# Two places where VectorE reads a sum: a change to the order of a fused attention and MLP kernel

## The chip, the cores and the metric

The kernel runs on one core of a Trainium2 chip. A core has five engines that run side by side, each with a queue of its own: TensorE (PE) multiplies matrices and writes into PSUM, VectorE (DVE) and ScalarE (ACT) read PSUM, GpSimd (POOL) works on the on-chip memory SBUF alone, and SyncE (SP) here only issues transfers. The metric is the device time of one execution in microseconds (us), lower being better; the medians of several runs are compared. A profile is one further execution, recorded instruction by instruction.

## What is computed

One transformer block with adaptive layer norm: 2048 tokens of width 512, 32 query heads of width 16 that share one key and one value head, and an MLP of inner width 1376. Everything is float32 to the caller.

```python
mod = silu(c) @ w_mod                        # six rows of 512: sa, ca, ga, sb, cb, gb
h = layernorm(x) * (1 + ca) + sa
q, k, v = h @ wq, h @ wk, h @ wv             # 32 heads of 16; one k, one v
p = softmax(q k^T / 4)                       # 32 x 2048 x 2048
x = x + ga * ((p v) @ wo)
h = layernorm(x) * (1 + cb) + sb
x = x + gb * (gelu(h @ w1 + b1) @ w2 + b2)
```

## The kernel before

**Units and passes.** The 2048 tokens are cut into eight blocks of 256, and each block into eight units of four heads, which makes 64 units. The loop at the end of the program goes through the units, with four passes for each unit: 256 passes in all. For one unit the softmax needs the row maximum first (a pass over all scores with nothing kept but the maximum) and the exponentials second. Both are made in the same loop, for different units: while unit u has its exponentials made, the maxima of a unit some way ahead are found.

**What a pass issues.** A pass has two half cycles. Each half cycle issues, in one order written by hand: four max products `m` (TensorE, 64 rows of the array, 512 columns, `Max.step`, L490), each followed by its reduction on VectorE (`mx`, L493); four score products `e` (L561), each followed by an exponential on ScalarE (`p`, L562); and the halves of the products of one filling batch (below, L183). Behind each half cycle stand sixteen small products `acc` that multiply the exponentials by the values (L573). In the first half cycle of a pass the max products use rows 64 to 127 of the array and the filling batch rows 0 to 63, and in the second the other way round, so that two products run side by side in the two halves of the array.

**PSUM banks.** The max products have three banks (`tag="m"`), the score products three (`e0` to `e2`), the accumulated `acc` one (`v`), and the filling products one (`x`). With one bank for the filling products, a new sum cannot start until the finished one has been read out of it.

**Filling batches.** All that is not attention is cut into batches that ride along in the half cycles. `take()` hands out a batch of up to twelve products; the batch is issued twice, half its contraction in each half cycle of the pass (`half`, L177 and L183). A sum is closed by a batch whose last product carries the stop flag (`batch[-1][4]`), and opened by one whose first product carries the start flag (`batch[0][3]`). There are five kinds of sums: query projections (`qps`, two batches, read by a VectorE copy, L441), output projections (`wops`, two batches, read by VectorE, L761), transposes (`tp`, one batch of four, read by a VectorE copy, L823, or by ScalarE, L828), the first MLP matrix (`w1ps`, one batch of twelve products of 256 columns, read by VectorE into `z`, L876) and the second (`w2ps`, six batches, read by VectorE, L928). When the last batch of a sum has been issued in the second half cycle, `resume()` (L1314) lets the job go on, and the job then issues the instruction that reads the finished sum. The reading instruction stands on VectorE's queue where `resume()` is called.

**Where the order comes from.** `issue()` takes several lists of steps with lengths, and always issues the step whose list has come least far. `mixture()` puts two lists alternately into one. `halves()` gives each product of a batch the length `ahead`, 0.75 for a full batch, and (6 - 0.5) / total for a smaller one, where total is the batch's size in products of 512 columns. A half cycle that opens a sum has an order of its own in the first half of a pass (the branch `if batch and batch[0][3]`, L1296 to L1300): two score products go first, and the max products follow each other more closely, while the batch starts later. All other half cycles with a batch use the order below it (L1302 and L1303).

**The maxima.** A unit's 32 max products are spread over four passes. After the last one, `put_max` (L504) finds the maximum of each row over its four columns (`mm`, L537), transposes it on VectorE (`turned`, L538), has GpSimd split it in two parts (`mt`, `mh`, `ml`, L532) and sends it with four transfers on SP's queue into the unit's query tile `qst` (L527); the score products of that unit wait for it. Time in the program is counted by `clock`, four ticks a pass. `later(n, fn)` puts a step off by n ticks; the transfers are issued four ticks after the reduction. Before the change the reduction itself is put off by `(0 - clock) % 4 + 1` ticks (L543), so it always stands behind the first half cycle of a pass.

Of the kernel before, what the change touches and what calls it, by code (L numbers as in the profile page):

```python
# [11 lines left out]
ALU = mybir.AluOpType  # L12
AX = mybir.AxisListType
# [19 lines left out]
BATCH = 6  # L33
# [14 lines left out]
def adaln_mqa_mlp(  # L48
# [416 lines left out]
    class Max:  # L465
# [14 lines left out]
        def has(self, s):  # L480
            return bool(self.todo[s])

        def step(self, s, **place):
            u, j, t, kc = self.todo[s].pop(0)
            T = blocks[units[u][0]][1] // P
            if u not in self.mx:
                self.mx[u] = att.tile([P, 4 * T, NKC], F32, name=f"mx{u}", tag="mx", bufs=2)
            m = psum.tile([P, 512], F32, name=f"m{u}_{j}_{t}_{kc}_{s}", **(place or dict(tag="m", bufs=3)))
            rows = slice(64 * s, 64 * s + 64)
            nc.tensor.matmul(m, qsts[u][rows, j, t * P:(t + 1) * P], ks[rows, kc * 512:(kc + 1) * 512],  # L490
                             start=True, stop=True)
            i = (s * 2 + j) * T + t
            nc.vector.tensor_reduce(out=self.mx[u][:, i, kc:kc + 1], in_=m, axis=AX.X, op=ALU.max)  # L493
            self.done += 1
            self.left[u] -= 1
            if self.left[u] == size[u] // 2 and u > 1 and u + 1 < NU:
                load_q(u + 1)
            if self.left[u] == 0:
                put_max(u, self.mx.pop(u))

    placed = set()
    mms = []
# [1 line left out]
    def put_max(u, mx):  # L504

        T = blocks[units[u][0]][1] // P
        qst = qsts[u]
        if not mms:  # L510
            for i in range(2):
                mms.append(att.tile([P, 32], F32, name=f"mm{i}"))
                nc.gpsimd.memset(mms[i], 0.0)
        mm = mms[u % 2]
        turned = att.tile([P, 32], F32, name=f"turned{u}", tag="turned", bufs=2)
        if u == 0:
            pad(att, 256, "pad7")
        mt = att.tile([4 * T, P], F32, name=f"mt{u}", tag="mt", bufs=2)
        mh = att.tile([4 * T, P], F32R, name=f"mh{u}", tag="mh", bufs=2)
        ml = att.tile([4 * T, P], F32R, name=f"ml{u}", tag="ml", bufs=2)  # L520

        def send():
            for s in range(2):
                for r, src in ((48, mh), (49, ml)):
                    dst = qst[64 * s + r:64 * s + r + 1].rearrange("p j (t n) -> p (j t) n", n=P)
                    ring = nc.scalar if u == 0 and s else nc.sync
                    ring.dma_start(out=raw(dst), in_=raw(src[2 * T * s:2 * T * (s + 1), :].unsqueeze(1)))  # L527
            placed.add(u)

        def gather():  # L530
            for g in range(0, P, 32):
                nc.gpsimd.tensor_scalar(out=mt[:, g:g + 32], in0=turned[g:g + 4 * T, :], scalar1=1.0, scalar2=0.0,  # L532
                                        op0=ALU.mult, op1=ALU.add)
            split(mh, ml, mt, nc.gpsimd, nc.gpsimd)

        def reduce():
            nc.vector.tensor_reduce(out=mm[:, :4 * T], in_=mx, axis=AX.X, op=ALU.max)  # L537
            nc.vector.transpose(out=turned, in_=mm)  # L538
            later(MAX_WAIT[0], gather)
            later(MAX_WAIT[1], send)  # L540


        later((0 - clock[0]) % 4 + 1, reduce)  # L543

    ptiles = {}
    accs = {}
# [527 lines left out]
    def resume():  # L1074

        go_on(holder[0])
# [187 lines left out]
    for u in range(NU):  # L1264
        for K in range(0, steps[u], 2):
            goal = lead[u] + (lead[u + 1] - lead[u]) * (K + 2) / steps[u]
            goal = min(goal, first[u + QBUFS] if u + QBUFS < NU else first[NU])
            n = max(0, 2 * round((goal - mp.done) / 2))

            def maxes(s, n, first_=1.0):  # L1270
                return [(1.0 if i else first_, lambda: mp.step(s)) if mp.has(s) else (0.0, lambda: None) for i in range(n)]

            def exps(s, which):
                return [(1.0, lambda K=K, j=j, bank=bank: sexp(u, K, j, s, bank)) for K, j, bank in which]

            def halves(batch, s):

                total = products(batch)
                ahead = AHEAD if total > BATCH - 0.5 else (BATCH - 0.5) / total
                return [(ahead * products([one]), lambda one=one: half(one, s)) for one in batch]  # L1280

            def plain(s, K, t, n, banks):

                a, b_, c_, d = banks
                one = mixture(exps(s, [(K, 0, a), (K, 1, c_)]), maxes(s, n))
                other = maxes(t, n)
                if not holder and mp.has(t) and n > 1:
                    other[-1] = 1.0, lambda: mp.step(t, tag="x", bufs=1)
                issue(one, exps(t, [(K, 0, b_)]) + other + exps(t, [(K, 1, d)]))

            X, Y = K, K + 1
            due()
            batch = take() if behind else None
            if batch and batch[0][3]:  # L1296

                one = mixture(maxes(1, n // 2), exps(1, [(X, 0, 1), (X, 1, 2)]))
                issue(one, exps(0, [(X, 0, 0)]) + halves(batch, 0))
                issue(exps(1, [(Y, 0, 0)]))  # L1300
            elif batch:
                issue(mixture(maxes(1, n // 2, 0.0), exps(1, [(X, 0, 0), (X, 1, 1), (Y, 0, 2)])),  # L1302
                      halves(batch, 0) + exps(0, [(X, 0, 0)]))  # L1303
            else:
                plain(1, X, 0, (n + 2) // 4, (1, 2, 0, 1))
            clock[0] += 1
            due()
            if behind:
                end_step(*behind)
            clock[0] += 1  # L1310
            due()
            if batch:
                issue(mixture(maxes(0, n // 2, 0.0), exps(0, [(X, 1, 0), (Y, 0, 1), (Y, 1, 2)])),
                      halves(batch, 1) + [(0.0, resume)] + exps(1, [(Y, 1, 0)]))  # L1314
                advance()
            else:
                plain(1, Y, 0, n // 4, (2, 0, 1, 2))
            clock[0] += 1
            due()
            end_step(u, X)  # L1320
            behind = (u, Y)
            clock[0] += 1
            if state["mods"] and state["q"] == 0 and w2H is None:
                w2H = att.tile([P, NF, D], F32R, name="w2H", tag="bigH")
                w2L = att.tile([P, NF, D], F32R, name="w2L", tag="bigL")
                preps["w2"] = prep_w2()
            if clock[0] >= prepared[0] + PREP and weights and weights[0] in preps:
                prepared[0] = clock[0]
                if next(preps[weights[0]], 0) == 0:
                    weights.pop(0)  # L1330
# [51 lines left out]
```

## Time and profile before

| | us |
|---|---|
| median of 3 runs | 1605.31 |
| lowest and highest of them | 1603.88, 1605.53 |
| the profiled execution, its own time | 1604.68 |
| its span, first to last instruction | 1602.5 |
| granted TensorE clock, mean | 0.995 of full speed |
| half cycles in its loop | 512 |

A row of the profile that groups instructions gives line, engine, operation, what is written and read, shapes, how many, then the busy time in all, the mean of one in ns, and the engine's idle time before them with the instruction that ended it. A row of a timeline gives the start in us from the span's start, the length, the engine, the operation and how many have been merged into the row; a bracket gives the idle time of that engine before the row and what ended it. PEld is TensorE's loading of weights, which overlaps its products, and waits of a product are mostly seen there. A row of a window table gives the window, its length, the busy time of each engine with its instructions, then the granted clock.

### The profile page before, as it was taken

The numbers are of one execution on the slowest core, as the hardware profiler recorded it, in microseconds if no ns is written. First come the engines' busy times: TensorE is split into PE (matmuls) and PEld (weight loads), VectorE is DVE, ScalarE is ACT, GpSimd is POOL, SyncE is SP. The second block draws the span as 40 slices with busy tenths as digits, with TensorE's granted clock in tenths as the row PEclk, the third lists the DMA queues.
The fourth block names the chain that finished last, engine by engine and source line by source line (L and its number), as shares of the span: only waits on it lengthen the run. The fifth ranks groups of instructions, "written<-read, shape, count | busy, mean of one in ns | idle before, by whom it ended". The sixth has DMA issues, their size and how long they took to land.

```text
span 1602.5 us, 41474 instructions
## 1 busy us (share of the span) xinstructions
PE 1572.6 (98%) x16369; PEld 1018.9 (64%) x16369; DVE 1407.6 (88%) x2473; ACT 1213.7 (76%) x2393; POOL 666.6 (42%) x1176
## 2 busy tenths in 40 slices
PE   6999999999999999999999999999999999999998
PEld 3466665557665666657666676657666676656667
DVE  6899999899999998999989998899999998999615
ACT  5577777678777887778877887778877887778853
POOL 4445444647422571246421462244612473225711
PEclk8999999999999999999999999999999999999999
DMA  7236312313021220303112120302112120212231
GB/s 251 80 108 212 108 68 71 125 32 107 16 94 35 67 68 26 101 19 106 32 50 78 53 84 22 106 14 97 42 40 86 45 95 19 100 33 63 80 134 72
DMA packets 83126, 121.63 MB, mean 76 GB/s; under 512 B 19614, under 2 KB 56222, under 8 KB 82676
## 3 DMA queue, kind: packets, MB, share of 16 engines
q1 hardware_dynamic: 82916, 118.97, 22.6%
q8 instruction: 130, 2.13, 0.6%
q14 instruction: 64, 0.52, 0.1%
q10 hardware_dynamic: 16, 0.00, 0.0%
HBM read 91.13 MB, written 27.27 MB: 74 GB/s over the span
## 4 chain that ended last, share of the span: by engine, by line
PE 90%; DVE 6%; ACT 2%; DMA 1%; issue 0%; POOL 0%; SPq 0%; ACTq 0%; DVEq 0%; POOLq 0%
PE acc L573 30%; PE m L490 25%; PE e L561 17%; PE w1ps L183 7%; DVE mx L493 4%; PE w2ps L183 3%; PE w2ps L177 1%; PE qps L183 1%; PE wops L183 1%; PE w1ps L177 1%; ACT p L562 1%; PE kps L159 1%; PE tp L183 1%; ACT h L828 0%; PE modr L279 0%
## 5 line engine op out<-in xcount | busy, mean ns | idle before, releaser
L493 DVE TENSOR_REDUCE mx<-m 128x1 f32<-128x512 f32 x2048 | 1273.2, 681 | 118.4 <-PE m L490 92.1
L562 ACT ACTIVATE p<-e 128x512 f32<-128x512 f32 x2048 | 1070.7, 600 | 289.4 <-PE e L561 220.5
L490 PE MATMUL m<-ks,qst 64*128 64x512 f32 x2048 | 812.7, 428 | 6.1 <-ACT ks L393 2.4
L561 PE MATMUL e<-qst,ks 64*128 64x512 f32 x2048 | 740.9, 413 | 6.7 <-DMA qst<-ml 5.2
L573 PE MATMUL acc<-p,va 128*32 128x256 f32 x8192 | 548.5, 385 | 0.0
L490 PEld LDWEIGHTS m<-ks,qst 64*128 64x128 f32 x2048 | 362.8, 184 | 226.1 <-DVE mx L493 108.5
L561 PEld LDWEIGHTS e<-qst,ks 64*128 64x128 f32 x2048 | 352.3, 184 | 85.4 <-ACT p L562 56.2
L573 PEld LDWEIGHTS acc<-p,va 128*32 128x32 f32 x8192 | 214.0, 109 | 223.2 <-issue 119.9
L183 PE MATMUL w1ps<-h2H,w1t 64*128 64x256 f32 x1232 | 228.9, 282 | 0.0
L532 POOL TENSOR_SCALAR mt<-turned 8x32 f32<-8x32 f32 x256 | 53.4, 208 | 400.7 <-DVE turned L538 388.7
L183 PEld LDWEIGHTS w1ps<-h2H,w1t 64*128 64x128 f32 x1232 | 189.3, 185 | 0.0
L183 PE MATMUL w1ps<-h2L,w1t 64*128 64x256 f32 x616 | 169.5, 275 | 0.0
L183 PE MATMUL w2ps<-w2H,gL 64*128 64x512 f32 x286 | 118.4, 414 | 0.0
L183 PE MATMUL w2ps<-w2L,gH 64*128 64x512 f32 x286 | 117.2, 410 | 0.0
L183 PE MATMUL w2ps<-w2H,gH 64*128 64x512 f32 x286 | 115.8, 405 | 0.0
L183 PEld LDWEIGHTS w1ps<-h2L,w1t 64*128 64x128 f32 x616 | 113.8, 185 | 0.0
L881 POOL TENSOR_SCALAR tt<-tt 128x256 f32<-128x256 f32 x77 | 31.2, 405 | 164.3 <-ACT tt L880 95.0
L134 POOL TENSOR_TENSOR gL<-z,gH 128x256 fp32r<-128x256 f32 x77 | 56.9, 739 | 6.4
L882 POOL TENSOR_TENSOR tt<-tt,z 128x256 f32<-128x256 f32 x77 | 56.8, 737 | 6.4
L892 POOL TENSOR_TENSOR z<-tt,z 128x256 f32<-128x256 f32 x77 | 56.2, 730 | 6.0
L891 POOL TENSOR_TENSOR tt<-tt,z 128x256 f32<-128x256 f32 x77 | 56.4, 732 | 0.0
L183 PEld LDWEIGHTS w2ps<-w2H,gH 64*128 64x128 f32 x286 | 52.8, 184 | 0.6
(188 smaller groups left out, 1461.2 us busy)
## 6 DMA issues: line engine op xcount, KB each, us to landing
w1t<-dw SPq DMA_DIRECT2D x82, 512.0 KB
qst<-dq SPq DMA_DIRECT2D x384, 32.0 KB
do<-oc SPq DMA_DIRECT2D x64, 128.0 KB
dw<-w1s SPq DMA_DIRECT2D x11, 512.0 KB
xt<-in_A_x_dram SPq DMA_DIRECT2D x4, 1024.0 KB
dq<-qH SPq DMA_DIRECT2D x16, 256.0 KB
dq<-qL SPq DMA_DIRECT2D x16, 256.0 KB
x<-in_A_x_dram SPq DMA_DIRECT2D x8, 512.0 KB
```

The costliest lines, as they stand in the source:

```text
L134: eng_l.tensor_tensor(out=dst_l, in0=src, in1=raw(dst_h), op=ALU.subtract)
L177: nc.tensor.matmul(ps, a, b_, start=first_, stop=last_)
L183: nc.tensor.matmul(ps, a[rows], b_[rows], start=first_ and s == 0, stop=last_ and s == 1)
L490: nc.tensor.matmul(m, qsts[u][rows, j, t * P:(t + 1) * P], ks[rows, kc * 512:(kc + 1) * 512], start=True, stop=True)
L493: nc.vector.tensor_reduce(out=self.mx[u][:, i, kc:kc + 1], in_=m, axis=AX.X, op=ALU.max)
L532: nc.gpsimd.tensor_scalar(out=mt[:, g:g + 32], in0=turned[g:g + 4 * T, :], scalar1=1.0, scalar2=0.0, op0=ALU.mult, op1=ALU.add)
L561: nc.tensor.matmul(e, ks[rows, kt * P:(kt + 1) * P], rhs, start=True, stop=True)
L562: nc.scalar.activation(ptiles[u, K][:, j, s, :], e, AF.Exp, scale=0.25)
L573: nc.tensor.matmul(accs[u][32 * cidx:32 * cidx + 32, :], va[:, kt, :], rhs, start=kt == 0, stop=kt == NKT - 1)
L882: nc.gpsimd.tensor_tensor(out=tt, in0=tt, in1=z, op=ALU.mult)
L891: nc.gpsimd.tensor_tensor(out=tt, in0=tt, in1=z, op=ALU.mult)
L892: nc.gpsimd.tensor_tensor(out=z, in0=tt, in1=z, op=ALU.add)
```

## The change

Three things are changed.

1. The order of its own for a half cycle that opens a sum is taken out. Such half cycles now use the order of all the others.
2. In the second half cycle of a pass whose batch closes a sum, the reduction of the third max product (index 2) is not issued with its product but held, and issued after `resume()`. VectorE's order in that half cycle was: reductions 1, 2, 3, reading of the sum, reduction 4. Now it is: reductions 1, 2, reading of the sum, reductions 3, 4. For small closing batches (the transposes) `ahead` becomes (6 - 1.5) / total, so that `resume()` comes ahead of the fourth max product; there the reading stood behind all four reductions before. What hung on the held reduction (loading the next query tile, `put_max`) goes along with it.
3. For the units of the first two blocks (`u < 2 * NQ`, sixteen units), the reduction in `put_max` is issued at once and not put off. What follows it (GpSimd's split, the transfers) keeps its distance in ticks and so moves ahead with it, by three ticks. From the third block on nothing changes there.

```diff
-        def step(self, s, **place):
+        def step(self, s, hold=None, **place):
...
-            nc.vector.tensor_reduce(out=self.mx[u][:, i, kc:kc + 1], in_=m, axis=AX.X, op=ALU.max)
+
+            def reduce():
+                nc.vector.tensor_reduce(out=self.mx[u][:, i, kc:kc + 1], in_=m, axis=AX.X, op=ALU.max)
+                self.left[u] -= 1
+                if self.left[u] == size[u] // 2 and u > 1 and u + 1 < NU:
+                    load_q(u + 1)
+                if self.left[u] == 0:
+                    put_max(u, self.mx.pop(u))
+
             self.done += 1
...
+            if hold is None:
+                reduce()
+            else:
+                hold.append(reduce)
...
-        later((0 - clock[0]) % 4 + 1, reduce)
+        if u < 2 * NQ:
+            reduce()
+        else:
+            later((0 - clock[0]) % 4 + 1, reduce)
...
-            def maxes(s, n, first_=1.0):
-                return [(1.0 if i else first_, lambda: mp.step(s)) if mp.has(s) else (0.0, lambda: None) for i in range(n)]
+            def maxes(s, n, first_=1.0, held=None):
+                return [(1.0 if i else first_, lambda i=i: mp.step(s, held if i == 2 else None)) if mp.has(s) else (0.0, lambda: None)
+                        for i in range(n)]
...
-                ahead = AHEAD if total > BATCH - 0.5 else (BATCH - 0.5) / total
+                ahead = AHEAD if total > BATCH - 0.5 else (BATCH - (1.5 if batch[-1][4] else 0.5)) / total
...
-            if batch and batch[0][3]:
-
-                one = mixture(maxes(1, n // 2), exps(1, [(X, 0, 1), (X, 1, 2)]))
-                issue(one, exps(0, [(X, 0, 0)]) + halves(batch, 0))
-                issue(exps(1, [(Y, 0, 0)]))
-            elif batch:
+            if batch:
                 issue(mixture(maxes(1, n // 2, 0.0), exps(1, [(X, 0, 0), (X, 1, 1), (Y, 0, 2)])),
                       halves(batch, 0) + exps(0, [(X, 0, 0)]))
...
-                issue(mixture(maxes(0, n // 2, 0.0), exps(0, [(X, 1, 0), (Y, 0, 1), (Y, 1, 2)])),
-                      halves(batch, 1) + [(0.0, resume)] + exps(1, [(Y, 1, 0)]))
+
+                reduces = [] if batch[-1][4] else None
+
+                def go_on_():
+                    resume()
+                    for fn in reduces or ():
+                        fn()
+
+                issue(mixture(maxes(0, n // 2, 0.0, reduces), exps(0, [(X, 1, 0), (Y, 0, 1), (Y, 1, 2)])),
+                      halves(batch, 1) + [(0.0, go_on_)] + exps(1, [(Y, 1, 0)]))
```

No instruction is added or taken away on any engine; the change moves instructions against each other.

More of the change, by code (lines that the diff above doesn't have):

```diff
@@ L492, in step @@
             i = (s * 2 + j) * T + t
-            nc.vector.tensor_reduce(out=self.mx[u][:, i, kc:kc + 1], in_=m, axis=AX.X, op=ALU.max)
-            self.done += 1
[L495 to L499, printed above, removed]
+            def reduce():
[5 more added lines that the diff above has]
+                    put_max(u, self.mx.pop(u))
+            self.done += 1
+            if hold is None:
+                reduce()
+            else:
+                hold.append(reduce)
     placed = set()
```

## The prediction, made before the changed kernel was run

> **What bounds the kernel now.** I read the page's first lines and its chain of waits first.
>
> ```profile
> span 1602.5 us, 41474 instructions
> PE 1572.6 (98%) x16369; PEld 1018.9 (64%) x16369; DVE 1407.6 (88%) x2473; ACT 1213.7 (76%) x2393; POOL 666.6 (42%) x1176
> ...
> PE 90%; DVE 6%; ACT 2%; DMA 1%; issue 0%; POOL 0%; SPq 0%; ACTq 0%; DVEq 0%; POOLq 0%
> ```
>
> TensorE sets the end, so the 512 half cycles of the loop are what is to be shortened, and a share of busy time cannot say which. I then read the timeline for the start of each half cycle (its first max product) and put windows over them. The window's first number is the length of a half cycle.
>
> ```profile
> 109.86:112.70 2.84, 2.84 (x34) 1.70 (x30) 2.70 (x7) 2.06 (x4) 2.49 (x7) 1.00 0.84 301
> 112.70:115.56 2.86, 2.86 (x34) 1.88 (x30) 2.50 (x5) 2.10 (x4) 2.06 (x3) 1.00 0.28 78
> 115.56:118.47 2.91, 2.91 (x34) 1.91 (x30) 2.53 (x5) 2.17 (x5) 0.00 (x0) 1.00 0.14 36
> 118.47:121.48 3.01, 3.01 (x34) 1.98 (x30) 3.01 (x6) 2.14 (x4) 2.65 (x4) 1.00 0.41 140
> 677.25:680.28 3.03, 3.03 (x34) 1.99 (x31) 3.03 (x7) 2.15 (x4) 0.00 (x0) 1.00 0.00 0
> ...
> 699.40:702.39 2.99, 2.99 (x36) 1.70 (x33) 2.99 (x6) 2.12 (x4) 1.43 (x2) 1.00 0.02 5
> 702.39:705.24 2.85, 2.85 (x37) 1.92 (x33) 2.40 (x5) 2.44 (x5) 0.00 (x0) 1.00 0.13 46
> 705.24:708.51 3.27, 3.08 (x37) 1.73 (x33) 3.18 (x7) 2.28 (x4) 2.23 (x4) 1.00 0.00 0
> ...
> 754.50:757.35 2.85, 2.85 (x40) 2.02 (x37) 2.70 (x8) 2.08 (x5) 2.41 (x8) 1.00 0.05 14
> 757.35:760.28 2.93, 2.93 (x40) 2.13 (x36) 2.93 (x5) 2.78 (x6) 2.68 (x6) 1.00 0.47 167
> ...
> 780.48:783.41 2.93, 2.93 (x34) 1.66 (x30) 2.93 (x5) 2.78 (x6) 2.69 (x6) 1.00 0.01 2
> ...
> 814.89:817.90 3.01, 3.01 (x33) 1.75 (x30) 3.01 (x6) 2.13 (x4) 0.00 (x0) 1.00 0.23 87
> ```
>
> The first four rows are the four half cycles of a query projection and the next one's start: 2.84 and 2.86 in the middle, 2.91 for the one that closes the sum, and 3.01 for the one that opens the next. The openings of the other kinds stand out too: output projection 3.03, the two transposes 2.99 and 3.27 (beside 2.85), first MLP matrix 2.93 (beside 2.85), second 2.93 and 3.01. The clock is 1.00 in all, so these are waits and not throttling. Where the 3.01 comes from is seen in VectorE's timeline and in that of the weight loads.
>
> ```profile
> 109.86 0.17 DVE L537 TENSOR_REDUCE mm<-mx 128x8 f32<-128x32 f32 x1
> 110.14 0.21 DVE L538 STREAM_TRANSPOSE turned<-mm 128x32 f32<-128x32 f32 x1
> ...
> 116.09 1.89 DVE L493 TENSOR_REDUCE mx<-m 128x1 f32<-128x512 f32 x3 [0.38 <-PE m L490]
> 117.90 0.68 DVE L441 COPY q<-qps 128x512 f32<-128x512 f32 x1
> 118.50 3.07 DVE L493 TENSOR_REDUCE mx<-m 128x1 f32<-128x512 f32 x5
> ```
>
> ```profile
> 118.47 0.18 PEld L490 LDWEIGHTS m<-ks,qst 64*128 64x128 f32 x1 [0.41 <-issue]
> ...
> 118.63 0.18 PEld L183 LDWEIGHTS qps<-bigH,wqH 64*128 64x128 f32 x1
> ...
> 119.83 0.18 PEld L490 LDWEIGHTS m<-ks,qst 64*128 64x128 f32 x1
> ```
>
> The sum is read out at 117.90 to 118.58, behind three reductions, so its bank comes free 0.11 us after the opening half cycle has begun; the order of its own starts the batch at 118.63 to allow for that. But its max products stand closer together, and the fourth one needs the bank of the first, whose reduction is the second of the run of five: 118.50 + 2 x 3.07/5 = 119.73. The product starts at 119.83, 0.10 later, with a score product still behind it. The half cycle ends late for the sake of VectorE, not of work on TensorE.
>
> **The change, part by part: openings.** Each sum costs one opening. Their number is in the groups of VectorE's reading instructions.
>
> ```profile
> L876 DVE TENSOR_SCALAR z<-w1ps,b1c 128x256 f32<-128x256 f32 x77 | 36.5, 474 | 3.8 <-PE w1ps L183 3.8
> ...
> L928 DVE TENSOR_TENSOR ot<-w2ps,x 128x512 f32<-128x512 f32 x16 | 10.9, 681 | 23.6 <-PE w2ps L183 15.9 <-PE w2ps L177 7.8
> L761 DVE TENSOR_TENSOR x<-wops,x 128x512 f32<-128x512 f32 x16 | 10.9, 680 | 0.8 <-PE wops L177 0.8
> ...
> L441 DVE COPY q<-qps 128x512 f32<-128x512 f32 x14 | 9.5, 679 | 0.0
> L823 DVE COPY tc<-tp 128x512 f32<-128x512 f32 x7 | 4.7, 678 | 0.0
> ```
>
> That is 77 first-matrix sums, 14 each of the second matrix and the output projection (two of the sixteen belong to the last block, behind the loop), 14 query projections, and 14 transposes (seven read by VectorE, seven by ScalarE): 133 openings. In the changed kernel they have the order of ordinary half cycles. What they then cost hangs on two things.
>
> First, the bank. The sum is read behind two reductions: the run of three starts at 116.09 and takes 0.63 each, so VectorE is free at 117.35. The sum's last product must be there as well.
>
> ```profile
> 116.91 0.40 PE L183 MATMUL qps<-bigL,wqH 64*128 64x512 f32 x1
> ...
> 117.07 0.41 PE L490 MATMUL m<-ks,qst 64*128 64x512 f32 x1
> ```
>
> It ends at 117.31, so VectorE waits for nothing and the bank is free at about 118.03, 0.44 before the opening begins at 118.47. Second, the fourth max product. The two reductions pushed behind the reading end where four ended before (one reading and four reductions in either order), so the opening's first reduction still ends near 119.73 and the bank is there at 119.83. In an ordinary half cycle the fourth product comes 117.07 - 115.56 = 1.51 after the start, here at 119.98. That is 0.15 to spare. So I take an opening at 2.86, the ordinary first half cycle of a pass with six products, for all kinds (low end 2.84, high end 2.91, the neighbours above):
> query projections 14 x (3.01 - 2.86) = 2.1; output projections 14 x (3.03 - 2.86) = 2.4; transposes 7 x (2.99 - 2.86) + 7 x (3.27 - 2.86) = 3.8; first matrix 77 x (2.93 - 2.86) = 5.4; second 7 x (2.93 - 2.86) + 7 x (3.01 - 2.86) = 1.5. Together 15.2 us gained. With 2.84 it is 2.7 more, with 2.91 it is 6.7 less.
>
> **The half cycle behind an opening** loses a rest: 109.86 takes 2.84 behind a long opening, 115.56 takes 2.91 behind an ordinary one, with the same six products. How much of the 0.07 comes back is not seen in this trace; the ends are 0 and 133 x 0.07 = 9.3 us. I take 0.01 each, 1.3 us lost, since most of the 133 have twelve short products, and these end a pass at 2.85.
>
> **The maxima of the first two blocks.** One wait in the trace is large.
>
> ```profile
> 277.57:280.18 2.61, 2.61 (x29) 1.36 (x26) 2.61 (x6) 2.06 (x4) 2.00 (x3) 1.00 0.30 89
> 280.18:286.55 6.37, 2.69 (x29) 1.29 (x25) 3.11 (x6) 2.07 (x4) 2.65 (x4) 1.00 0.36 118
> 286.55:290.28 3.73, 3.73 (x24) 2.19 (x25) 2.48 (x4) 2.08 (x4) 3.56 (x4) 0.55 0.21 45
> ```
>
> ```profile
> 272.34 0.45 POOL L134 TENSOR_TENSOR ml<-mt,mh 8x128 fp32r<-8x128 f32 x1
> ```
>
> ```profile
> 273.63 0.33 SPq L682 DMA_DIRECT2D drs<-rsum  x1
> ...
> 281.64 0.64 SPq L527 DMA_DIRECT2D qst<-mh  x1
> ```
>
> ```profile
> 286.55 0.89 PE L561 MATMUL e<-qst,ks 64*128 64x512 f32 x2 [3.68 <-DMA qst<-ml]
> ```
>
> The maximum of a unit in the second block is ready on GpSimd at 272.79, but its transfers stand on SP's queue behind the fetch of the first block's results, which waits for 273.63's transfer, and go out at 281.64 only. TensorE waits, and after the wait runs at a granted clock of 0.55 for a half cycle. Cost: 6.37 + 3.73 - 2 x 2.61 = 4.9 us. In the changed order these four transfers are ahead of 273.63 on SP's queue. The maximum is made four reductions (2.5 us) earlier, so they go out near 270.4; from issue to the product took 286.55 - 281.64 = 4.9, so the tile is there near 275.3, long before 281.8 + 1.0. What is queued behind them on SP (weights, the fetch) waits until 270.4 for GpSimd, and 273.63 was later than that anyway. I take the whole 4.9 as gained; the low end is 3.8, if the slow clock has another cause.
>
> This part has a price. Before, `mm` and `turned` ran at 109.86 to 110.35, in VectorE's idle time at the start of a second half cycle. Now they stand behind the fourth reduction, and where the half cycle closed a sum they fall into an opening. That is so for seven openings of query projections, one of a transpose and three of the first matrix: eleven. They take 0.49, of which the next reduction overlaps some 0.07: 0.42. Less the 0.15 to spare, the fourth max product is 0.27 late: 11 x 0.27 = 3.0 us lost (ends: 0, and 11 x 0.42 = 4.6).
>
> **The sum.** 15.2 + 4.9 - 1.3 - 3.0 = 15.8 us, from the profiled execution's own 1604.68 to 1588.9. That execution lay 0.6 below the median of the runs, 1605.31, so I forecast 1589.
>
> **A rule against it.** In one opening, that of the second transpose, the trace shows what a late bank does.
>
> ```profile
> 706.12 0.18 PEld L183 LDWEIGHTS tp<-ident,xh 64*128 64x128 f32 x1 [0.59 <-PE e L561]
> ...
> 706.15 0.18 PEld L490 LDWEIGHTS m<-ks,qst 64*128 64x128 f32 x1
> ```
>
> The max product behind the transposes could have run, its bank was free, and yet it started only with them, 0.9 us after the half cycle began. The Trainium skill (PSUM — Partial Sum Buffer, section Engine vs sequencer instructions) states this as a rule: VectorE's queue is strictly first in, first out, and matmuls start and complete in program order. By that rule the reading moved forward holds up reductions 3 and 4 whenever the sum is late, and the batch moved forward holds up three max products whenever the bank is late; the trace agrees with the second half, and the first half is the third rival below.
>
> **Rivals.**
> *The rest is given back.* If all half cycles with six products ran at 2.91 and the twelve-product pairs kept their 2.93 + 2.85, the projections and the first matrix would gain nothing (4 x 2.91 = 11.6 against 2.84 + 2.86 + 2.91 + 3.01 = 11.6), and there would remain 3.8 + 1.5 + 4.9 - 3.0 = 7.2 us: 1598. For it: 2.84 comes only behind an opening. Against: it takes a slowing that the trace shows in at most two half cycles running.
> *It doesn't do what it says.* VectorE has as much to do as before in the two half cycles, so if the fourth max product is what binds, and not the bank, openings stay near 3.0 and only 4.9 - 3.0 remains: 1603 to 1605, no change. Against: 0.15 to spare in the count above.
> *Slower: the sum is late.* VectorE stands waiting for the sum's last product, ahead of two reductions. Beyond the 0.15 to spare, each opening grows by that wait. All openings would have to lose 0.12 (15.8/133) before the gain is gone, so it decides from a wait of 0.27. With 0.41, the longest idle time quoted at a half cycle's start, it costs 133 x 0.26 = 35 us: about 1620. Against: the count gives 117.31 for the last product and 117.35 for VectorE.
>
> **Chances.** The forecast 0.62; given back 0.19; not what it says 0.07; the sum late 0.12. For this kernel 0.2%, 3.2 us, is about what can be told from no change. Faster by more: 0.62 + 0.19 + a little of the third, 0.82. Within: 0.06. Slower: 0.12. Range: the low ends of the costs give 1604.7 - 15.2 - 2.7 - 4.9 = 1582; upward it takes in the first rival, 1598, with 2 us for its own spread: 1600. What is left out is the last two rivals, 0.19.
>
> **What would show it.** Windows over an opening should read about 2.86, with the first filling product's weights loaded within 0.1 of the start and no wait for VectorE before the fourth max product; the reading of a sum should begin 0.6 earlier in its half cycle, without idle time before it. There should be no wait for `ml` near 281, and no clock under 1.00 there. Eleven openings of the first two blocks should stand out at about 3.1. The forecast is wrong if VectorE shows idle time before its readings, or if half cycles that were 2.84 become 2.91.

## The result, and the profile after

The changed kernel takes 1595.12 us (median of 4 runs, 1593.97 to 1597.31) against 1604.89 us for the kernel before (4 runs): a ratio of 0.9941, 95% interval 0.9924 to 0.9959. It is 9.8 us faster; 15.8 were forecast. The profiled execution is the slowest of the four, 1597.31 us, 7.4 below the profiled one of before.

First the page of the changed kernel: its first lines and the chain of waits.

```profile
span 1595.0 us, 41579 instructions
PE 1569.6 (98%) x16369; PEld 1020.0 (64%) x16369; DVE 1410.1 (88%) x2473; ACT 1203.6 (75%) x2393; POOL 668.1 (42%) x1176
...
PE 92%; DVE 4%; ACT 2%; DMA 1%; POOL 0%; issue 0%; SPq 0%; ACTq 0%; DVEq 0%; POOLq 0%
```

VectorE's share of the chain fell from 6% to 4%. The page counts 105 instructions more than before (41474), though each engine's count of products, reductions and so on is the same: the program as built has more semaphore instructions, most of them ahead of ScalarE's exponentials (211 against 95). On TensorE's filling products there are 77 where there were 84; one group of these matters below. The windows over single half cycles, in the columns of the prediction:

```profile
107.64:110.99 3.35, 3.35 (x35) 2.07 (x31) 3.21 (x8) 2.15 (x4) 2.91 (x8) 1.00 0.82 266
...
116.68:119.58 2.90, 2.90 (x35) 1.91 (x31) 2.51 (x5) 2.16 (x5) 0.27 (x1) 1.00 0.42 124
119.58:122.49 2.91, 2.91 (x34) 1.88 (x30) 2.91 (x6) 2.15 (x4) 2.74 (x4) 1.00 0.57 188
...
284.94:287.56 2.62, 2.62 (x29) 1.35 (x25) 2.49 (x6) 2.07 (x4) 0.74 (x1) 1.00 0.54 159
307.38:311.88 4.50, 3.96 (x35) 1.97 (x31) 3.97 (x7) 2.29 (x4) 4.25 (x5) 1.00 0.77 287
493.08:495.98 2.90, 2.90 (x35) 1.87 (x31) 2.90 (x6) 2.14 (x4) 0.00 (x0) 1.00 0.00 0
...
703.60:706.45 2.85, 2.85 (x37) 1.78 (x33) 2.85 (x6) 2.08 (x4) 2.51 (x6) 1.00 0.00 0
723.46:726.31 2.85, 2.85 (x41) 2.02 (x37) 2.49 (x6) 2.71 (x7) 0.00 (x0) 1.00 0.20 63
755.09:758.02 2.93, 2.93 (x40) 2.09 (x36) 2.93 (x6) 2.43 (x6) 2.68 (x6) 1.00 0.51 173
```

119.58 is the opening of a query projection that was 3.01: now 2.91. 107.64 is one with `mm` and `turned` in it: 3.35. 703.60 is the second transpose, 3.27 before: 2.85. 493.08 is an output projection, 3.03 before. The wait for `ml` is gone: 284.94 stands where 286.55 stood, 2.62 instead of 3.73, and its clock is 1.00 instead of 0.55. 755.09 opens a sum of the first MLP matrix, and that is 2.93 as it was. And 307.38 is new: 4.50 where there were 3.01.

I grouped the half cycles by what they do (length: from one first max product to the next) and compared the two traces, from the loop's second pass on. In us:

- the two half cycles with the wait for `ml`: 4.9 gained, and 0.4 lost again in a half cycle at 290.16 (below);
- openings, with the cost of `mm` and `turned` taken out: 11.0 gained, of which transposes 4.1, output projections 1.8, first matrix 1.8, query projections 1.7, second matrix 1.6;
- `mm` and `turned` in eleven openings: 4.4 lost;
- the half cycles behind openings: 1.5 lost;
- the half cycle at 307 and the next one: 1.6 lost;
- all others: 0.3 lost.

The sum is 7.7, and this part is 7.7 shorter (1466.45 to 1458.78). Ahead of it, from TensorE's first product on, the changed kernel takes 0.5 longer (74.6 and 75.1). Counted from that first product to the loop's end, which is what "the loop" means in the lengths given below, it is 7.1 shorter (1541.0 to 1533.9). Three questions follow: why the 77 openings of the first matrix hardly gained, what the maxima cost, and what waits at 307.

**The first matrix.** A block has eleven sums of the first matrix, numbered f = 0 to 10 in the program. Two of their openings in the timeline of the weight loads, the first belonging to the third sum of a block, the second to a later one:

```profile
726.30 0.18 PEld L490 LDWEIGHTS m<-ks,qst 64*128 64x128 f32 x1 [0.41 <-DVE mx L495]
726.34 0.18 PEld L183 LDWEIGHTS w1ps<-h2H,w1t 64*128 64x128 f32 x1
...
755.09 0.18 PEld L490 LDWEIGHTS m<-ks,qst 64*128 64x128 f32 x1 [0.41 <-issue]
755.18 0.18 PEld L183 LDWEIGHTS w1ps<-h2H,w1t 64*128 64x128 f32 x1
```

The instructions of L183 between 755 and 758, grouped, have one kind more than those of 726:

```profile
L183 PEldq EVENT_SEMAPHORE  x1: 51/51/51, 755.1 to 755.1; - x1
```

The first filling product of a sum from f = 3 on has two semaphores to wait for: VectorE's for the bank, and that of the transfer of its weights `w1t`, which no earlier instruction of TensorE has waited for. In this program the second wait is an instruction of its own, 0.051 us on TensorE's queue, and the product comes 0.09 behind the max product and not 0.04. The trace of before has this instruction in the same 56 openings, but there the order of its own started the batch later anyway. For f = 1 and 2 the bank alone is waited for (for f = 0 the bank and GpSimd, which makes `h2H`). In the later blocks the 12 openings with f = 1 or 2 take 2.844 on the mean (2.836 to 2.849), the 48 with f from 3 on 2.925; before, with the order of its own, both took 2.94.

**The wait at 307.** VectorE's timeline, and SP's queue:

```profile
305.01 1.29 DVE L495 TENSOR_REDUCE mx<-m 128x1 f32<-128x512 f32 x2 [0.37 <-PE m L490]
307.91 0.69 DVE L771 TENSOR_TENSOR x<-wops,x 128x512 f32<-128x512 f32 x1 [1.61 <-PE m L490]
308.52 1.28 DVE L495 TENSOR_REDUCE mx<-m 128x1 f32<-128x512 f32 x2
```

```profile
298.45 0.66 SPq L534 DMA_DIRECT2D qst<-mh  x1
...
300.57 0.57 SPq L534 DMA_DIRECT2D qst<-ml  x1
302.32 0.34 SPq L1059 DMA_DIRECT2D w2f<-in_B_w_dram  x1
302.71 0.43 SPq L738 DMA_DIRECT2D x<-in_A_x_dram  x1
```

The reading of the output projection's sum adds the input `x`. The profile puts VectorE's 1.61 us down to a max product, but that was long done; `x` was issued at 302.71 only, behind a load of `w2f` and the four transfers of unit 10's maxima. Loads of `w2f` stand ahead of it in the kernel before too; the four transfers were moved ahead of it by the third part of the change (before, `x` was issued at 297.25 and they from 299.25 on). The reading stands in front of reductions 3 and 4 now, so these waited too.

**The half cycle at 290.16** takes 2.97 where 2.60 stood. It is the first with max products of a new unit. The last transfer of that unit's query tile was issued on SP's queue at 289.34 and landed at 290.95; TensorE's semaphore instruction for it ends at 290.98, and the first max product comes at 291.00, 0.84 behind the half cycle's start. In two_units, where this transfer goes out 1.8 us ahead of the half cycle, the product comes 0.22 behind the start and the half cycle takes 2.60.

### The profile page after: what moved, and what is told of

The parts are those of the page before. It is cut to its first block, busy times and chain, and to the rows that moved or that the text cites. A ratio compares the mean times of both kernels' runs of the same rounds, so it can differ in the third digit from the quotient of the medians.

```text
span 1595.0 us, 41579 instructions
## 1 busy us (share of the span) xinstructions
PE 1569.6 (98%) x16369; PEld 1020.0 (64%) x16369; DVE 1410.1 (88%) x2473; ACT 1203.6 (75%) x2393; POOL 668.1 (42%) x1176
## 4 chain that ended last, share of the span: by engine, by line
PE 92%; DVE 4%; ACT 2%; DMA 1%; POOL 0%; issue 0%; SPq 0%; ACTq 0%; DVEq 0%; POOLq 0%
PE acc L583 31%; PE m L490 25%; PE e L571 18%; PE w1ps L183 7%; PE w2ps L183 4%; DVE mx L495 3%; PE wops L183 1%; PE w2ps L177 1%; PE qps L183 1%; PE w1ps L177 1%; ACT p L572 1%; PE kps L159 1%; PE tp L183 1%; ACT h L838 0%; PE modr L279 0%; DMA wm<-in_w_mod_dram 0%
## 5 line engine op out<-in xcount | busy, mean ns | idle before, releaser
L571 PEld LDWEIGHTS e<-qst,ks 64*128 64x128 f32 x2048 | 365.9, 184 | 86.5 <-ACT p L572 59.0
L183 PE MATMUL w1ps<-h2H,w1t 64*128 64x256 f32 x1232 | 235.1, 287 | 0.0
L183 PEld LDWEIGHTS w1ps<-h2H,w1t 64*128 64x128 f32 x1232 | 184.2, 185 | 0.0
L183 PE MATMUL w1ps<-h2L,w1t 64*128 64x256 f32 x616 | 169.7, 276 | 0.0
L183 PE MATMUL w2ps<-w2H,gH 64*128 64x512 f32 x286 | 117.8, 412 | 0.0
L183 PE MATMUL w2ps<-w2H,gL 64*128 64x512 f32 x286 | 117.3, 410 | 0.0
L183 PE MATMUL w2ps<-w2L,gH 64*128 64x512 f32 x286 | 117.3, 410 | 0.0
L183 PEld LDWEIGHTS w1ps<-h2L,w1t 64*128 64x128 f32 x616 | 113.5, 184 | 0.0
L183 PEld LDWEIGHTS w2ps<-w2H,gH 64*128 64x128 f32 x286 | 52.7, 184 | 0.6
```

The costliest lines, as they stand in the source:

```text
L183: nc.tensor.matmul(ps, a[rows], b_[rows], start=first_ and s == 0, stop=last_ and s == 1)
L571: nc.tensor.matmul(e, ks[rows, kt * P:(kt + 1) * P], rhs, start=True, stop=True)
```

## The experiments

Each ratio is that to the kernel before, run again beside them; its median was 1604.89 in the first row's runs, 1605.56 and 1605.36 in the others'. Where the intervals of two rows overlap, the half cycles of the traces decide, not the medians.

| kernel | us, median | ratio | 95% interval |
|---|---|---|---|
| changed | 1595.12 | 0.9941 | 0.9924 to 0.9959 |
| no_early_maxima | 1598.15 | 0.9958 | 0.9945 to 0.9970 |
| early_maxima_alone | 1605.50 | 1.0004 | 0.9995 to 1.0013 |
| one_unit | 1596.50 | 0.9942 | 0.9928 to 0.9955 |
| spread_waits | 1593.01 | 0.9923 | 0.9910 to 0.9935 |
| order_alone | 1599.08 | 0.9959 | 0.9945 to 0.9973 |
| own_order | 1608.99 | 1.0026 | 1.0015 to 1.0036 |
| two_units | 1591.38 | 0.9917 | 0.9904 to 0.9930 |
| mended | 1589.21 | 0.9897 | 0.9883 to 0.9910 |

### Where the second wait stands: spread_waits

```diff
     def half(one, s):
...
+        mul = nc.tensor.matmul(ps, a[rows], b_[rows], start=first_ and s == 0, stop=last_ and s == 1)
+        if last_ and s == 1 and id(ps) in next_w1:
+            tc.add_manual_dep(mul.ins, next_w1.pop(id(ps)).ins.name,
+                              mybir.DependencyInfo(mybir.DependencyClass.Sync, mybir.DependencyReason.DATA), reason="next w1")
...
```

`next_w1` holds, for each sum of the first matrix, the transfer that loads the `w1t` of the sum behind it.

> The changed kernel; the wait for the weights of the next sum of the first MLP matrix stands at the last filling product of the sum before, and no longer at the first product of the opening, which waits for the bank alone. No instruction is added or moved. Theory (the second wait is what makes 56 openings of the first matrix 2.93 and not 2.85): they fall to 2.85, with the first filling product 0.04 and not 0.13 behind the half cycle's start, 56 x 0.09 = 5 us less, 1590. Rival (these openings wait for the bank, whichever semaphores stand there): they stay at 2.93, 1595. Second rival (the weights land so late that the wait was real): the closing half cycles grow by as much, 1595.

The same opening as the one at 755.09 above, its window and its weight loads:

```profile
754.74:757.58 2.84, 2.84 (x40) 2.01 (x37) 2.84 (x6) 2.33 (x6) 2.59 (x6) 1.00 0.52 172
```

```profile
754.73 0.18 PEld L496 LDWEIGHTS m<-ks,qst 64*128 64x128 f32 x1 [0.41 <-issue]
754.74 0.18 PEld L186 LDWEIGHTS w1ps<-h2H,w1t 64*128 64x128 f32 x1
```

The page counts 41523 instructions, 56 fewer, and the openings from f = 3 on fell from 2.925 to 2.853, those with f = 1 or 2 stayed (2.843). The half cycles ahead of them and behind them stayed at 2.85 to 2.86, so the weights had landed and both rivals are out. The loop is 3.5 shorter, although the stretch ahead of its second pass is 0.8 longer in this trace, and the median is 2.1 lower; 5 were expected, since I had reckoned with 0.09 for each and the mean loss was 0.07. The intervals of this row and the changed kernel's overlap; the openings show the effect.

### The order, and the reading ahead, each alone: order_alone, own_order

```diff
-                ahead = AHEAD if total > BATCH - 0.5 else (BATCH - (1.5 if batch[-1][4] else 0.5)) / total
+                ahead = AHEAD if total > BATCH - 0.5 else (BATCH - 0.5) / total
...
-                reduces = [] if batch[-1][4] else None
+                reduces = None
```

> The changed kernel without the reading ahead: openings have the order of ordinary half cycles, but a finished sum is read behind the third reduction again, and its last products come as late as before. Theory (order and reading are needed together): the bank comes free about 0.1 us after the opening has begun, as the trace of before shows for a query projection (118.58 against 118.47); TensorE stands at the first filling product until then, and openings of sums with a reading of 0.68 us are about 3.0 (query projections, first transposes, second matrix, output projections), those of the first matrix, with a reading of 0.48, 2.90 to 2.95: 2 to 8 us above the changed kernel, 1597 to 1603. Rival (the order was the whole cost): openings as in the changed kernel, 1595.

Windows of order_alone over the openings of a query projection, the second transpose and the first matrix, then its weight loads at the first of them:

```profile
118.76:121.75 2.99, 2.99 (x34) 2.03 (x30) 2.99 (x6) 2.14 (x5) 2.61 (x4) 1.00 0.57 186
...
703.13:706.42 3.29, 3.10 (x36) 1.79 (x33) 3.21 (x7) 2.19 (x4) 2.24 (x4) 1.00 0.00 0
755.02:757.97 2.95, 2.95 (x41) 2.11 (x37) 2.95 (x5) 2.61 (x6) 2.71 (x6) 1.00 0.48 173
```

```profile
118.76 0.18 PEld L490 LDWEIGHTS m<-ks,qst 64*128 64x128 f32 x1 [0.41 <-DVE mx L495]
118.87 0.19 PEld L571 LDWEIGHTS e<-qst,ks 64*128 64x128 f32 x1
118.94 0.18 PEld L183 LDWEIGHTS qps<-bigH,wqH 64*128 64x128 f32 x1
```

The filling product waits for the bank until 0.18 after the start, as expected, the output projections stay at 2.99 and 3.05, and the second transposes keep their 3.27. But the theory holds in part only. The first transposes fell to 2.84 and the second matrix to 2.83 and 2.87 where 3.0 was expected, with nothing read ahead. And the first matrix is as in the changed kernel (2.845 for f = 1 and 2, 2.924 from 3 on); its reading takes 0.48 only, and the order alone is enough there. The medians put the reading ahead at 4 us (1599.1 to 1595.1), the loops of the two traces at 2; most of it is 0.42 in each second transpose, and none of it in the first matrix.

own_order puts the order of its own back and keeps the reading ahead:

```diff
-            if batch:
+            if batch and batch[0][3]:
+
+                one = mixture(maxes(1, n // 2), exps(1, [(X, 0, 1), (X, 1, 2)]))
+                issue(one, exps(0, [(X, 0, 0)]) + halves(batch, 0))
+                issue(exps(1, [(Y, 0, 0)]))
+            elif batch:
```

> The changed kernel with the order of its own in the openings, as before: the sum is still read ahead of the third reduction. Theory (in that order the fourth max product comes too early for VectorE, however early the bank is free): openings stay as they were before, 3.0 for query projections and 2.93 for the first matrix, those with mm in them longer; what is gained is the 4.5 for ml alone, less what mm and x1 cost: 1603 to 1607. Rival (the bank alone was the cost): 1595 as the changed kernel.

```profile
119.10:122.23 3.13, 3.13 (x35) 2.07 (x31) 3.13 (x6) 2.17 (x4) 2.96 (x4) 1.00 0.67 199
```

```profile
116.73 1.29 DVE L495 TENSOR_REDUCE mx<-m 128x1 f32<-128x512 f32 x2 [0.38 <-PE m L490]
118.04 0.69 DVE L441 COPY q<-qps 128x512 f32<-128x512 f32 x1
118.64 3.67 DVE L495 TENSOR_REDUCE mx<-m 128x1 f32<-128x512 f32 x6
```

1609.0, slower than before and above the range: the opening takes 3.13, where the kernel before took 3.01. The rows of VectorE say why. Before, the reading began at 117.90, 0.08 ahead of the end of the run of three reductions (116.09 + 1.89 = 117.98): consecutive instructions overlap. Here it begins at 118.04, 0.02 behind the end of the run of two (118.02), for it waits for the sum. So 0.10 is lost, and the six reductions behind it are late by that. Together with early_maxima_alone below, which has the order of its own and no reading ahead, four kernels with the early maxima cover both parts: with the order of its own, reading ahead costs 3.5 us (1605.5 to 1609.0); with the new order, which asks for the fourth max product later, it gains (1599.1 to 1595.1).

### The maxima: no_early_maxima, early_maxima_alone, one_unit, two_units

The first puts the third part of the change back, the second makes that part alone:

```diff
-        if u < 2 * NQ:
-            reduce()
-        else:
-            later((0 - clock[0]) % 4 + 1, reduce)
+        later((0 - clock[0]) % 4 + 1, reduce)
```

> The changed kernel with the maxima of every unit put off again, as before. Theory (the sum of the traces): against the changed kernel (1595.1) the wait for ml in the second block comes back (+4.5), the eleven openings with mm and turned in them lose these (-4.4), and the wait of 1.5 for x1 at 307 goes, since x1 is loaded ahead of the maxima of unit 10 again (-1.6): about 1593.6, and the profile shows 6.4 and 3.7 for the two half cycles near 280 and no opening of a query projection above 3.0. Rival (the prediction's own prices, mm at 3.0 and nothing at x1): 1595.1 + 4.9 - 3.0 = 1597.

> The kernel before, with nothing but the maxima of the first two blocks made at once. Theory: the wait for ml goes (-4.5), mm and turned fall into openings that VectorE already makes late and are paid in full there (11 x 0.42 = +4.6), x1 comes late as in the changed kernel but its reading has all its reductions ahead of it (0 to +1.5): 1605 to 1606.5, no change. Rival (the prediction's prices): 4.9 gained and 3.0 lost, 1603.

Windows of no_early_maxima over the two half cycles with the wait for `ml`, and the one that was 4.50:

```profile
278.85:284.86 6.01, 2.68 (x28) 1.29 (x25) 3.12 (x6) 2.07 (x4) 2.56 (x4) 0.95 0.36 116
284.86:288.90 4.04, 4.04 (x25) 2.21 (x26) 2.48 (x4) 2.08 (x4) 3.87 (x4) 0.50 0.23 52
309.08:311.96 2.88, 2.88 (x34) 1.87 (x30) 2.88 (x6) 2.12 (x4) 1.29 (x2) 1.00 0.38 140
```

The wait is back with its slow clock, and the half cycle with `x` takes 2.88. The openings of the query projections take 2.87 to 2.92, none above 3.0 (the first pass of the loop, 3.11, apart). The steps came as the theory had them, but the time was 4.5 above it and nearer to the rival's. The wait cost 5.4 over three slow half cycles, and seven half cycles elsewhere are 0.2 to 0.9 longer (see the end). The rest is in no half cycle: the profiled executions of the two kernels differ by 0.7 only, their medians by 3.0.

Made alone on the kernel before, the early maxima bring nothing, 1.0004. Its windows show the wait gone and both prices:

```profile
107.93:111.48 3.55, 3.55 (x34) 2.12 (x30) 3.41 (x8) 2.17 (x5) 2.98 (x7) 1.00 0.74 238
286.66:289.26 2.60, 2.60 (x28) 1.33 (x24) 2.48 (x6) 2.06 (x4) 0.74 (x1) 1.00 0.45 147
308.97:313.03 4.06, 3.56 (x34) 2.05 (x30) 3.59 (x6) 2.28 (x4) 3.81 (x5) 1.00 0.77 279
```

`mm` and `turned` cost 3.55 - 3.01 = 0.54 in that opening (0.44 to 0.46 in the five others like it), and `x` is late without the reading ahead as well.

Then I made the maxima at once only where they are waited for.

```diff
-        if u < 2 * NQ:
+        if u == 9:
```

> The changed kernel with the maxima made at once for unit 9 alone, the one whose tile TensorE waited for, and put off for the others. Theory: no wait for ml, ten or eleven openings fall from 3.1-3.4 to about 2.9 (-4.4), x1 is loaded before the maxima of unit 10 and the half cycle at 307 falls from 4.5 to about 3.0 (-1.6): 1595.1 - 6 = about 1589. Rival (the openings of the first two blocks are long for another reason, and the maxima of other units than 9 are late too): a wait near 280 or no change, 1594 to 1600.

That was a miss, 1596.5. The openings did fall to 2.9, but the wait moved on by one unit. The window, and TensorE's row in it:

```profile
306.44:312.39 5.95, 3.30 (x34) 1.99 (x30) 3.37 (x7) 2.15 (x4) 4.88 (x5) 1.00 0.34 105
```

```profile
309.58 0.47 PE L571 MATMUL e<-qst,ks 64*128 64x512 f32 x1 [2.65 <-DMA qst<-ml]
```

This is the first score product of unit 10. Its transfers went out from 301.58 on, behind `w2f`, `x` and three weight loads. Counted from the loop's second pass that is 215.2 us, and 215.8 in the kernel before; but there TensorE had lost 4.9 us to unit 9's wait and came later. So both units need it, and then `x` has to go out earlier:

```diff
-        if u < 2 * NQ:
+        if u in (9, 10):
...
         def fetch():
+            if b == 0:
+                load_x1(b)
...
```

`load_x1` is the load of `x`, which stood in `fetch_rest`; for the first block it is now issued ahead of the fetch of the block's results.

> The changed kernel with the maxima made at once for units 9 and 10 alone, and the x of the first block's output loaded ahead of the fetch of its results (with unit 9 alone, TensorE waited 2.7 us for the ml of unit 10 in its place, and x1 was late in the changed kernel). Theory: no wait for ml in either place, no idle VectorE before the first reading of an output projection, the openings of the first two blocks near 2.9: 1595.1 - 4.4 - 1.5 = 1589. Rival (a wait follows at unit 11, 2 to 3 us): 1592. Rival (x1's transfer delays the fetch and the maxima): 1594 to 1597.

```profile
108.80:111.67 2.87, 2.87 (x34) 1.88 (x30) 2.87 (x6) 2.11 (x4) 2.70 (x4) 1.00 0.85 272
...
283.58:286.20 2.62, 2.62 (x29) 1.35 (x26) 2.50 (x6) 2.06 (x4) 0.63 (x2) 1.00 0.62 203
...
305.69:308.58 2.89, 2.89 (x35) 1.88 (x31) 2.89 (x6) 2.13 (x4) 2.80 (x3) 1.00 0.47 162
```

Neither wait is left, and the half cycles of the first two blocks' work are together 6.2 us shorter than in the changed kernel (about 6 expected). The rest of the loop is the same to 0.1: a few half cycles are 0.2 to 0.3 longer, others shorter. But the stretch ahead of the loop's second pass is 1.5 longer, so the loop gains 4.6; the medians differ by 3.7, to 1591.4 and not 1589.

### All together: mended

The edits of two_units and spread_waits.

> The kernel two_units with the waits for the first matrix's weights moved as in spread_waits. Theory: the two gains add, since they lie in different half cycles (only three of the first two blocks' openings are in both): 1589 less 3.5 of the trace of spread_waits (1530.4 against 1533.8 for the loop), about 1585. Rival: what is gained in the first blocks goes in a later wait, 1590 or more.

1589.2 us, ratio 0.9897; its interval lies wholly below that of the changed kernel. The loop is 7.8 shorter than the changed kernel's, and the median 5.9. It missed its own 1585: of the loop's 4.6 from two_units and 3.5 from spread_waits nearly all is there (8.1 against 7.8), but I had counted the gain of two_units at its expected size. This is the fastest version, 16 us below the kernel before, which is what the prediction had hoped of the change itself; it gets there by other edits, so that does not bear the prediction out.

## Why the prediction was right, and where its sum was not

The forecast was 1589, and the range 1582 to 1600 holds the 1595.1. The direction and the main mechanism were right; two terms were mis-sized and two waits were not foreseen. The range reaches up to 1600 for the sake of the rival that the rest is given back, which did not come true. That the result lies inside says little of the sum: the prediction's own price for openings of 2.91 throughout, 6.7 less, would have given 1595.6, but the openings came out between 2.84 and 2.99 on the mean of a kind, and other terms made up the difference.

- **Openings, +15.2 forecast, 11.0 measured.** For the transposes (4.1 against 3.8) and the second matrix (1.6 against 1.5, of which 0.4 in one opening behind the last max products) the term was right, and query projections (1.7 against 2.1) and output projections (1.8 against 2.4) came near. The step that failed is "What they then cost hangs on two things": it named the bank and the fourth max product, and took 2.86 for all kinds. For 56 openings of the first matrix a third thing decides, the second wait of the first filling product. The term for the first matrix was 5.4 and came out at 1.8; spread_waits, which moves that wait alone, gave about 56 x 0.07 = 3.9 of it back.
- **"0.15 to spare".** This was the count for the fourth max product, and it was nothing. It set the start of a product (117.07) against that of a weight load (119.83). The weight load of the product at 117.07 is this one, in the kernel before:

```profile
116.98 0.18 PEld L490 LDWEIGHTS m<-ks,qst 64*128 64x128 f32 x1
```

It starts 1.42 behind its half cycle, so the load in the opening would be due at 119.89, with 0.06 to spare. That was lost as well, as the rows of an ordinary opening in the changed kernel show (the sum's last product, its reading, the reductions, and the fourth max product of the half cycle that starts at 119.57):

```profile
118.03 0.39 PE L183 MATMUL qps<-bigL,wqH 64*128 64x512 f32 x1
...
118.53 0.69 DVE L441 COPY q<-qps 128x512 f32<-128x512 f32 x1
119.13 3.67 DVE L495 TENSOR_REDUCE mx<-m 128x1 f32<-128x512 f32 x6
...
121.06 0.18 PEld L490 LDWEIGHTS m<-ks,qst 64*128 64x128 f32 x1
```

The sum ends at 118.42 and is read at 118.53, behind the end of the two reductions ahead of it (118.50) and not overlapping it: the 0.10 that own_order shows. The prediction had VectorE wait for nothing here. The six reductions start every 0.60 and take 0.68 each, so the third ends at 119.13 + 2 x 0.60 + 0.68 = 121.01, and the load that needs its bank starts at 121.06, 1.49 behind the start and not 1.42. So query projections came to 2.91 and not 2.86.
- **The maxima in eleven openings, 3.0 forecast, 4.4 measured.** The mechanism and the eleven places were right; with nothing to spare, query projections pay all of it (3.35 against 2.91, 0.44), the three of the first matrix 0.24 each. two_units, which takes them out of these openings, shows 2.87 there.
- **The wait for `ml`, 4.9 forecast, 4.9 measured.** With the half cycle at 290.16, where the max products of the next unit wait for their query tile, 4.5 remain. The four transfers were forecast at 270.4 and went out at 271.97. The slow clock belongs to the wait: it is 1.00 wherever the wait is gone and 0.50 where no_early_maxima brings it back.
- **"What is queued behind them on SP".** I followed the queue for unit 9 alone. The same step for unit 10 puts its four transfers ahead of the load of `x`: 1.6 lost, not in the sum. two_units shows it gone; one_unit, where `x` again goes ahead of unit 10's transfers, shows the reading without a wait and TensorE waiting for the transfers instead.
- **The half cycle behind an opening, 1.3 forecast, 1.5 measured**, but not 0.01 on each: those behind an output projection's opening went from 2.84 to 2.93 (1.1 of the 1.5), the others hardly moved.

**The rivals.** The rest was not given back: behind the openings of the first matrix the trace has 2.85 as before. That the fourth product binds and not the bank holds for query projections in part, as above. The sum is hardly late: at query projections by the lost overlap of 0.1, and in the loop VectorE stands idle 0.04 us or less before its readings, apart from two of the first matrix (0.33 and 0.36 us at 577 and 954, with openings of 3.06 and 3.09 behind them), one at 1508, behind the last max products, where it has nothing else to do and waited as long before (3.6 and 3.8), and the one at 307. At 307 it was not TensorE's sum that was late but the other operand, and the cost was the one that the rule in the prediction names: the Trainium skill (PSUM — Partial Sum Buffer, section Engine vs sequencer instructions) has VectorE's queue strictly first in, first out, and the trace of the changed kernel agrees, with reductions 3 and 4 behind a reading that waited 1.61 us.

## What to carry to other kernels

When work is moved ahead on an in-order engine, list every operand that the moved instruction waits for, not only the one for which it is moved: a second semaphore, or a load issued later on another queue, takes the gain back. When a transfer is moved ahead of others, follow each of these to its reader, and look also at the next unit, which a removed wait brings closer. A slack has to be worked out from starts of one kind, product against product or weight load against weight load (here 0.09 us apart), and it is no better than the overlap of neighbouring instructions, which one that has to wait loses (here 0.1 us).

## What the runs showed of the hardware

A second wait is dear or free by where it stands. At the first filling product of an opening the extra semaphore instruction (0.051 us) cost 0.07 us of the half cycle. The first max product of a unit waits for five semaphores (VectorE's and those of the four transfers of its query tile). The instructions for these waits stand at the end of the half cycle ahead, and they do not lengthen it: of the closing half cycles of the first matrix in the changed kernel, the first block's left out, the 18 ahead of a new unit take 2.85 on the mean, the 47 others 2.85 as well. That these waits stand behind the accumulating products, which keep TensorE busy meanwhile, is a reading that no run tested.

After the waits of 3.68 and 3.33 us for `ml` the granted clock was 0.55 and 0.50 in the next half cycle (before, no_early_maxima); after the 2.65 us in one_unit it stayed at 1.00 in that half cycle and the next. Where between these the clock begins to fall no run shows.

Two things stay open. In the stretch ahead of the loop's second pass the granted clock differs from profile to profile at the same place, here mended and then the changed kernel:

```profile
45.00:50.00 5.00, 5.00 (x26) 3.15 (x24) 4.19 (x8) 4.69 (x8) 4.92 (x5) 0.70 0.47 144
50.00:55.00 5.00, 5.00 (x20) 2.89 (x18) 3.19 (x6) 3.26 (x6) 4.17 (x5) 0.61 0.18 75
```

```profile
45.00:50.00 5.00, 5.00 (x30) 3.22 (x29) 4.82 (x9) 4.82 (x9) 4.92 (x6) 1.00 0.61 192
50.00:55.00 5.00, 5.00 (x22) 2.81 (x23) 4.42 (x8) 2.70 (x4) 4.92 (x5) 1.00 0.07 26
```

The time from TensorE's first product to the loop's second pass was 74.6 us before, 75.1 in the changed kernel, 76.7 in mended and 77.4 in one_unit. And in several kernels, above all in the four without the early maxima for sixteen units but with the new order (no_early_maxima, one_unit, two_units, mended), a few half cycles, much the same ones in each, are longer, mostly by 0.2 to 0.4, with a pause right behind their first max product that no semaphore in the profile ends. One of them in one_unit:

```profile
728.20 0.18 PEld L490 LDWEIGHTS m<-ks,qst 64*128 64x128 f32 x1 [0.41 <-DVE mx L495]
728.51 0.18 PEld L571 LDWEIGHTS e<-qst,ks 64*128 64x128 f32 x1
```

The record of transfers holds a hint. At four of these places (374.27, 728.20, 866.34 and 1003.37 in one_unit) a transfer of 8 KB of instructions starts 0.1 to 0.2 us ahead of the half cycle in each of those four kernels, and in the six others, which do not pause there, none does. Other transfers of this kind pass without a pause, so this is not shown to be the cause.

What two_units and mended miss of their expectations, 2 and 4 us, is in part the longer stretch ahead of the loop's second pass (1.5 us in both traces). The rest lies between the medians and the profiled executions; what causes either was not tried.
